# Chunks 0 and 1 of the first expert in turns of four blocks of f, with a later due time for the second group of weights, and another order of the steps between the two experts

## The chip, the cores and the metric

The kernel runs on one core of one Trainium2 chip. The metric is the device time of one execution in microseconds; the median of three runs stands for the kernel, and less is better. The engines are TensorE (PE, the matrix products; its weight loads are shown as PEld), VectorE (DVE), ScalarE (ACT), GpSimd (POOL) and SyncE (SP), which here issues every DMA. Each engine works through its own queue in order.

## The reference

Two batches of 3008 x 256 numbers go through a two-dimensional Fourier transform, of which the real part is kept; the 6016 rows that come out pass through two experts one after the other.

```python
X = np.fft.fft(np.fft.fft(x, axis=1), axis=2).real        # (2, 3008, 256)
x = X.reshape(6016, 256)
h = x @ w_in;  g = h / (1 + exp(-h));  x = g @ w_out       # first expert: w_in 256 x 2048
h = x @ w_in2; g = max(h, 0) + alpha * min(h, 0)           # second expert, alpha per column
out = g @ w_out2
```

The weights come as float64. Everything else is float32.

## The kernel before

**Tiles.** For a real input the rows of the transform come in mirrored pairs, so that half of them, 1504 pairs per batch, are enough. The pairs of a batch are three chunks of 502 columns, six chunks in all (c = 0 to 5). The hidden dimension of 2048 is 16 blocks of 128 (f = 0 to 15). Products are done in fp32r, with every factor split into a high and a low part: high x high, low x high and high x low make three matmuls of one product. The high part is an ACT copy, the low part a subtraction on DVE or POOL.

**Start.** Stage A (`stage_a`, lines 250 to 306) transforms batch 0 along 64 points; its results go through DRAM (`store`, line 297, and `load_y`, line 314) to come back turned. The part of them that chunk 1 needs is stored by `rest(1)` and the part of chunk 2 by `rest(2)`. Stage B (`stage_b`, line 317) does the 47-point part in groups: the matmuls at line 327 fill a PSUM tile, ACT copies the high part of z (line 345), DVE subtracts the low part (line 347). Stage C (`stage_c`, line 351) makes from z the three operands of a chunk: even (ev), odd (od) and the column 128 (ny).

**Weights of the first expert.** They are converted in four groups of four blocks of f: `prep_w1(g)` for W_in, called i0 to i3, and `prep_o1(g)` for W_out, called o0 to o3. `to_f32` (line 174) makes float32 from the two halves of a float64 in one ACT pass (line 183) and four DVE passes (lines 187, 191, 195, 199) on 128 x 512; a group of W_in and a group of W_out have two such pieces each, so 8 DVE passes a group. Then POOL forms sum and difference of W_in (lines 427, 430), ACT makes high parts (lines 434, 452) and POOL low parts (lines 437, 456).

**Rounds.** The first expert runs in 96 rounds, one for each pair (c, f) in `ORDER`. A round issues `eo_mm(i)`: three matmuls for pe (even) and three for po (odd); then `mm2(i-2)`, the second product of the round two earlier (`LAG` = 2): 12 matmuls that add to four accumulators; then `silu_split(i)`: on DVE t = n * w128 + pe (line 570), hp = t + po (line 573) and t - po (line 574), on ACT two silu passes for each of hp and t (lines 577, 578), and `low1(i-1)`, the low parts gl (line 590), in the first 30 rounds both on POOL. When the next round has another chunk, `mm2` empties the four accumulators: by a copy if it is the chunk's first time (two on ACT, line 625, two on DVE, line 623), by an addition on DVE if it is not (four, line 621). Before, chunks 0, 1 and 2 take f 0 to 7 one after the other, then f 8 to 15; chunks 3 to 5 take all 16 at once.

**What sets the order.** `PLAN` gives each kind of side work a stretch of rounds (a, b); `put` spreads its steps evenly over it. A round's steps are issued after its own operations; `leash` ties them to operations of the round before, so that they are not taken earlier. A scheduler works through this order of the program and takes another instruction only where the next one isn't ready by its own reckoning; what it fixes is the order of each engine's queue. Of the tiles, `pm` (PSUM) has four buffers, shared by pe, po and the tiles of stages B and C, `pa` four for the accumulators, `big` twelve in SBUF for raw weights, y, z, the operands and results of a chunk.

**Passage.** The second expert works in 96 pairs n, of which the first two share their time with `mm2` of the last two rounds (lines 942 and 963). A pair's `outer`, `inner`, `seventh` and `fourth` are seven block products of a Strassen-like form, three matmuls of 252 columns each, into PSUM tiles that ACT and DVE empty (e at line 690, u at lines 708 and 714, h at lines 704, 709, 719), followed by the prelu and by `mm4(n-2)`. Its weights are converted during the first expert (`w2`, rounds 50 to 88), combined in `prep_ws` (ws0, ws1), and the second factor is finished in `prep_wo2(g)`: four ACT passes that multiply with a sign (line 542) and the split into high and low (lines 167, 168), for g = 0 to 3. `split_o1(t)` makes and splits the block sums of the first result: four differences (`forms`, line 650) and five splits (`halves`, lines 659, 660) with the low part on POOL.

Of the kernel before, what the change touches and what calls it, by code (L numbers as in the profile page):

```python
# [19 lines left out]
NF = DFF // 128  # L20
NPAIR = S // 2 + 1
CW = 502
NCB = 3
NC = B * NCB
LAG = 2
PLAN = {
# [6 lines left out]
}  # L33
W2_AHEAD = 2
HALF = 252
# [11 lines left out]
FOLD1 = "pppppppppppppppp"  # L47
LOW1 = "vvpvvvvv"
A_SPLIT = (0, 1)
F_PARTS = (0, 8, 16)  # L50
ORDER = [(c, f) for f0, f1 in zip(F_PARTS, F_PARTS[1:]) for c in range(NCB) for f in range(f0, f1)]
ORDER += [(c, f) for c in range(NCB, NC) for f in range(NF)]
WARM = 20
WARM0 = 8
# [67 lines left out]
def fft_moe_kernel(  # L122
# [12 lines left out]
    nc = tc.nc  # L135
# [95 lines left out]
    cx = wp.tile([128, 128], F32R, name="cx")  # L231
# [8 lines left out]
    LAST = {}  # L240
# [67 lines left out]
    def load_y(b, h, kh):  # L308
        w = (K_PARTS[kh + 1] - K_PARTS[kh]) // 2
        if (b, kh) not in Y:  # L310
            Y[b, kh] = big([96, 2, 6, 128], F32, f"y{b}_{kh}")
        src = YS[b, h, kh].rearrange("n (a j k) m -> j (n a) k m", a=4, j=2)
        for j in range(2):
            last = nc.sync.dma_start(Y[b, kh][48 * j : 48 * j + 48, h, :w, :], src[j])
        return last
# [71 lines left out]
    V2 = {}  # L387
# [11 lines left out]
    def load_half(key, src, i, at=None):  # L399
        if key not in RAW:  # L400
            RAW[key] = big([128, 1024, 2], U32, f"raw_{key}")
        at = i * 512 if at is None else at
        t = RAW[key].rearrange("p n t -> p (n t)")
        return nc.sync.dma_start(t[:, i * 1024 : i * 1024 + 1024], src[:, at : at + 512].bitcast(U32))
# [5 lines left out]
    def wo_tiles(lay, g):  # L410
        for j in range(2):
            WO[lay, g, j] = wp.tile([128, 4, 256], F32R, tag=f"wo{g}_{j}", name=f"wo{lay}_{g}_{j}")

    def load_w1(g):
        load_raw(f"i{g}", wi1[0, :, 512 * g : 512 * g + 512], wi1[1, :, 512 * g : 512 * g + 512])

    def load_o1(g):
        load_raw(f"o{g}", wo1[:, 1024 * g : 1024 * g + 1024])
# [112 lines left out]
        return steps  # L531

    def prep_wo2(g):
        def part(h):
            if h == 0:
                wo_tiles(2, g)
            o = (g % 2) * 1024 + h * 512
            v = V2["o", g // 2][:, o : o + 512]
            for q in range(2):
                f = 4 * g + 2 * h + q  # L540
                w = v[:, 256 * q : 256 * q + 256]
                nc.scalar.activation(w, w, AF.Copy, scale=fc[:, 2, f : f + 1])
            hi, lo = (WO[2, g, j].rearrange("p f e -> p (f e)")[:, h * 512 : h * 512 + 512] for j in range(2))
            split(hi, lo, v, nc.gpsimd)

        return [lambda: part(0), lambda: part(1)]


    ACC1 = {}
# [4 lines left out]
    def eo_mm(i):  # L554
        c, f = ORDER[i]
        g, fo = divmod(f, 4)
# [24 lines left out]
    def lo_pool(i):  # L581
        return i < LO_POOL or 52 <= i < 88

    def low1(i):
        if i < 0:
            return
        for s in range(2):
            hi, h = G[i, s]
            lo = work(F32R, f"gl{i}_{s}")
            LAST["gl", i] = (nc.gpsimd if s or lo_pool(i + 1) else nc.vector).tensor_tensor(  # L590
                lo, h, hi.bitcast(F32), op=ALU.subtract
            )
            G[i, s] = (hi, lo)

    def mm2(i, lbs=(0, 1)):
        c, f = ORDER[i]
        g, fo = divmod(f, 4)
# [38 lines left out]
    def split_o1(t):  # L636

        c, s = divmod(t, 2)
        b = lambda k, j: O1[c][:, 2 * s + k, (L, R)[j]]
        box = {}  # L640

        def forms(n):
            if n == 0:
                box["t"] = [work(F32, f"xt{t}_{j}", 2 * HALF) for j in range(2)]
            t1, t2 = box["t"][0][:, :HALF], box["t"][0][:, HALF:]
            t3, t4 = box["t"][1][:, :HALF], box["t"][1][:, HALF:]
            to, p, q = (
                (t1, b(0, 1), b(0, 0)), (t3, b(1, 1), b(0, 1)), (t2, b(1, 1), t1), (t4, b(1, 0), t2),
            )[n]
            nc.gpsimd.tensor_tensor(to, p, q, op=ALU.subtract)  # L650

        def halves(n):
            if n == 0:
                OS[t] = [big([128, 7, HALF], F32R, f"os{t}_{j}") for j in range(2)]
            hi, lo = OS[t]
            to = slice(n, n + 1) if n < 3 else slice(2 * n - 3, 2 * n - 1)
            src = b(*((0, 0), (1, 0), (1, 1))[n]) if n < 3 else box["t"][n - 3]
            hi, lo = (o[:, to, :].rearrange("p b n -> p (b n)") for o in (hi, lo))
            nc.scalar.activation(hi, src, AF.Copy)  # L659
            nc.gpsimd.tensor_tensor(lo, src, hi.bitcast(F32), op=ALU.subtract)  # L660

        return [lambda n=n: forms(n) for n in range(4)] + [lambda n=n: halves(n) for n in range(5)]
# [126 lines left out]
    if True:  # L789
        with tc.manual_schedule():  # L790
            zero = conv(F32, "zero")
            nc.vector.memset(zero[:, :256], 0.0)
            warm(zero[:, :128], zero[:, :256], WARM0)
            nc.vector.memset(sm, 0.0)
            nc.scalar.activation(sm[:1, :1], sm[:1, :1], AF.Silu)
            for j in range(len(PIECES) - 1):
                load_x(0, j, (PIECES[j + 1] - PIECES[j]) // 2)
                if j == 0:
                    nc.sync.dma_start(cs[:, :R0], cst[:, :R0])
            cc = conv(F32, "cc")  # L800
            for g in range(2):
                load_half("i0", wi1[g], g, 0)
                if g == 0:
                    nc.sync.dma_start(cc, cst[:, CD0:])
                    nc.sync.dma_start(w128_raw.rearrange("p n t -> p (n t)"), w128.bitcast(U32))
            nc.sync.dma_start(cs[:, R0:], cst[:, R0:CD0])
            fold, mm, rest = stage_a(0)
            (i00, _), (i01, after_i0) = prep_w1(0)
            for (h, i), n in zip(A_ORDER, A_WARM):
                if h == 0:  # L810
                    fold(i)
                mm(h, i)
                warm(cs[:, FA0 : FA0 + 128], cs[:, :256], n)
            load_half("o0", wo1, 0)
            for h in range(2):
                load_y(0, h, 0)
            load_half("o0", wo1, 1)
            load_w1(1)
            load_o1(1)
            warm(cs[:, FA0 : FA0 + 128], cs[:, :256], WARM)  # L820
            (s0, p0), (s1, p1) = prep_o1(0)
            w128_st = to_f32(lambda: w128_sb, ("w128", 0, NF), "w128")[1]
            run(i00[:4])
            run(i01[:2])
            run(w128_st[:1])
            nc.scalar.activation(ch, cc, AF.Copy)
            run(i00[4:])
            for ab in zip(i01[2:], w128_st[1:]):
                run(ab)
            run(w128_st[4:])  # L830
            nc.vector.tensor_tensor(cl, cc[:, : SG0 - CD0], ch.bitcast(F32)[:, : SG0 - CD0], op=ALU.subtract)
            for n, (st, pool) in enumerate(zip(after_i0, SUM0)):
                (st if callable(st) else st[pool == "v"])()
                if n == 2:
                    run(s0)
            b00, b01 = stage_b(0, 0), stage_b(0, 1)
            run(b00[:2])
            run(b01[:2])
            run(p0)
            run(s1[:EARLY_O0])  # L840
            run(stage_c(0, 0))
            rest(1)
            for h in range(2):
                load_y(0, h, 1)
            nc.sync.dma_start(alpha_sb, alpha)
            rest(2)
            for h in range(2):
                load_y(0, h, 2)
        n1 = NC * NF
        fold, mm, rest = stage_a(1)  # L850
# [8 lines left out]
        def put(a, b, steps):  # L859

            for j, st in enumerate(steps):
                plan.setdefault(a + (b - a) * j // len(steps), []).append(st)
# [45 lines left out]
            put(*PLAN[f"ws{pg}"], steps[:8])  # L908
            put(*PLAN[f"ws{pg}b"], steps[8:])
        for g in range(4):  # L910
            put(*PLAN[f"wo{g}"], prep_wo2(g))
        put(n1 - 5, n1 - 1, split_o1(0))

        for i in range(n1):
            pe, po = eo_mm(i)
# [103 lines left out]
```

## Time and profile before

| | |
|---|---|
| median of 3 runs | 976.97 us (976.53 to 977.37) |
| profiled execution, its own time | 975.78 us |
| span of the profiled execution | 974.0 us |
| PE busy | 953.6 us (98%) |
| DVE busy | 785.1 us (81%) |
| ACT busy | 709.3 us (73%) |
| POOL busy | 424.6 us (44%) |
| DMA | 37.06 MB, mostly in the first 75 us |

The profile is of one execution. Times are microseconds from the start of the span, if not marked ns. A line such as L590 is the line of the code that issued an instruction; `gl<-t,gh` says which tile is written from which. "idle before" is the time in which the engine had nothing to do ahead of an instruction, with the instruction that ended it. PEclk is the share of full speed that was granted to PE. PE's records overlap, since matmuls are pipelined, and a few of them can be missing.

### The profile page before, as it was taken

To read this page: it belongs to the slowest core of one execution; us is meant where nothing else is said; L and a number is where in the kernel's file an instruction comes from. 1 tells how busy PE (TensorE), PEld (TensorE's weight loads), DVE (VectorE), ACT (ScalarE), POOL (GpSimd) and SP (SyncE) were. 2 spreads that over 40 slices of the span, in tenths; PEclk is the share of its full clock that TensorE was granted. 3 is DMA by queue.
4 is the path that set the end of the run, shared out by engine and by line. 5 is a ranking of instruction groups with operands and counts; after the bars stand their busy time and mean duration, and the time that the engine had idled before them with its cause. 6 is when DMAs were issued, how large, how long until landed. Compare 5 with 4: busy or idle time off the path is not lost.

```text
span 974.0 us, 14393 instructions
## 1 busy us (share of the span) xinstructions
PE 953.6 (98%) x5186; PEld 821.7 (84%) x5186; DVE 785.1 (81%) x1319; ACT 709.3 (73%) x1410; POOL 424.6 (44%) x368
## 2 busy tenths in 40 slices
PE   8899999999999999999899999999999999999998
PEld 6578888788788888887789999999999999999997
DVE  5977888787696988997588787887878888787876
ACT  3557677575575757778788787888888888887875
POOL 2576889753257677799522131221222112131200
PEclk9989999999999999999999999999999999999999
DMA  8822000015101110100000000000000000000000
GB/s 269 284 78 87 1 1 22 22 28 174 44 1 60 44 61 27 44 1 1 1 1 22 1 22 23 1 22 1 23 22 1 22 1 22 22 1 22 1 23 21
DMA packets 16615, 37.06 MB, mean 38 GB/s; under 512 B 1824, under 2 KB 11296, under 8 KB 14880
## 3 DMA queue, kind: packets, MB, share of 16 engines
q1 hardware_dynamic: 16544, 36.15, 11.2%
q8 instruction: 40, 0.66, 0.3%
q14 instruction: 31, 0.25, 0.1%
HBM read 26.83 MB, written 9.31 MB: 37 GB/s over the span
## 4 chain that ended last, share of the span: by engine, by line
PE 87%; DVE 3%; POOL 3%; ACT 3%; issue 2%; DMA 0%; SPq 0%; POOLq 0%; DVEq 0%; ACTq 0%
PE a L772 27%; PE ac L674 20%; PE a L614 7%; PE a L616 7%; PE a L612 7%; PE b L674 3%; PE po L562 2%; PE po L564 2%; PE pe L562 2%; PE po L563 2%; PE pe L564 2%; PE pe L563 2%; POOL gl L590 2%; PE psb L327 1%; PE psa L283 1%
## 5 line engine op out<-in xcount | busy, mean ns | idle before, releaser
L772 PE MATMUL a<-gh,wo 128*128 128x502 f32 x768 | 268.2, 391 | 0.0
L772 PEld LDWEIGHTS a<-gh,wo 128*128 128x128 f32 x768 | 145.1, 189 | 23.3
L741 DVE SCALAR_TENSOR_TENSOR h<-h,fc,q 128x502 f32<-128x502 f32 x192 | 129.9, 676 | 38.0 <-ACT q L736 35.3
L590 POOL TENSOR_TENSOR gl<-t,gh 128x502 fp32r<-128x502 f32 x96 | 133.6, 1392 | 55.4 <-ACT t L578 44.5
L614 PE MATMUL a<-gl,wo 128*128 128x502 f32 x384 | 148.6, 396 | 4.0 <-POOL gl L590 2.9
L772 PE MATMUL a<-gl,wo 128*128 128x502 f32 x384 | 149.7, 391 | 0.0
L616 PE MATMUL a<-gh,wo 128*128 128x502 f32 x384 | 146.6, 392 | 0.0
L577 ACT ACTIVATE gh<-hp 128x502 fp32r<-128x502 f32 x96 | 59.8, 623 | 116.5 <-DVE hp L573 115.5
L752 DVE TENSOR_TENSOR gl<-h,gh 128x502 fp32r<-128x502 f32 x192 | 140.7, 733 | 0.1
L612 PE MATMUL a<-gh,wo 128*128 128x502 f32 x384 | 119.2, 393 | 2.4 <-ACT gh L577 2.3
L747 ACT ACTIVATE gh<-h 128x502 fp32r<-128x502 f32 x192 | 118.4, 617 | 2.1 <-DVE h L741 2.1
L590 POOL TENSOR_TENSOR gl<-hp,gh 128x502 fp32r<-128x502 f32 x65 | 90.1, 1386 | 68.1 <-ACT hp L578 66.5
L736 ACT ACTIVATE q<-h,fc 128x502 f32<-128x502 f32 x192 | 116.9, 609 | 2.8 <-DVE h L719 1.5
L650 POOL TENSOR_TENSOR xt<-o 128x252 f32<-128x252 f32 x24 | 16.7, 715 | 187.2 <-ACT q L736 149.8
L614 PEld LDWEIGHTS a<-gl,wo 128*128 128x128 f32 x384 | 73.1, 190 | 21.6 <-POOL gl L590 5.1
L570 DVE SCALAR_TENSOR_TENSOR t<-n,sm,pe 128x502 f32<-128x502 f32 x96 | 70.3, 732 | 25.5 <-PE pe L564 23.6
L612 PEld LDWEIGHTS a<-gh,wo 128*128 128x128 f32 x384 | 71.8, 189 | 18.7 <-ACT gh L577 4.0
L616 PEld LDWEIGHTS a<-gh,wo 128*128 128x128 f32 x384 | 73.1, 190 | 14.6
L772 PEld LDWEIGHTS a<-gl,wo 128*128 128x128 f32 x384 | 72.4, 189 | 7.6
L708 ACT ACTIVATE u<-ac 128x252 f32<-128x252 f32 x96 | 36.6, 381 | 54.2 <-PE ac L674 54.2
L573 DVE TENSOR_TENSOR hp<-t,po 128x502 f32<-128x502 f32 x96 | 64.5, 672 | 13.9 <-PE po L564 6.8
L660 POOL TENSOR_TENSOR os<-o,os 128x252 fp32r<-128x252 f32 x36 | 32.4, 912 | 92.4 <-ACT os L659 92.4
(191 smaller groups left out, 2294.0 us busy)
## 6 DMA issues: line engine op xcount, KB each, us to landing
out_t<-ot SPq DMA_DIRECT2D x24, 251.0 KB, 2.6
x<-in_xs SPq DMA_DIRECT2D x8, 512.0 KB, 5.4
raw_i<-in_wi SPq DMA_DIRECT2D x8, 512.0 KB, 6.2
raw_w<-in_wi SPq DMA_DIRECT2D x4, 1024.0 KB, 5.9
raw_w<-in_wo SPq DMA_DIRECT2D x4, 1024.0 KB, 4.8
raw_o<-in_wo SPq DMA_DIRECT2D x3, 1024.0 KB, 6.8
y<-ys SPq DMA_DIRECT2D x16, 144.0 KB, 3.4
x<-in_xs SPq DMA_DIRECT2D x2, 1024.0 KB, 4.7
```

Source lines behind the costliest of these rows:

```text
L570: nc.vector.scalar_tensor_tensor(t, E128[c], w128_sb[:, f : f + 1], pe, op0=ALU.mult, op1=ALU.add)
L573: nc.vector.tensor_tensor(hp, t, po, op=ALU.add)
L590: LAST["gl", i] = (nc.gpsimd if s or lo_pool(i + 1) else nc.vector).tensor_tensor(lo, h, hi.bitcast(F32), op=ALU.subtract)
L612: nc.tensor.matmul(ACC1[lb, s], hi, G[i, s][0], start=st, stop=False)
L614: nc.tensor.matmul(ACC1[lb, s], hi, G[i, s][1], start=False, stop=False)
L616: nc.tensor.matmul(ACC1[lb, s], lo, G[i, s][0], start=False, stop=sp)
L674: nc.tensor.matmul(to, w, x, start=start and q == 0, stop=q == 2, skip_group_check=True)
L736: nc.scalar.activation(h["q", i][:, to], source(n, part), AF.Abs, scale=coef(n, i, 1))
L741: nc.vector.scalar_tensor_tensor(h[f"h{i}"][:, to], source(n, part), coef(n, i, 0), h["q", i][:, to], op0=ALU.mult, op1=ALU.add)
L747: nc.scalar.activation(hi, H[n][f"h{i}"], AF.Copy)
L752: nc.vector.tensor_tensor(lo, H[n][f"h{i}"], G[n, i][0].bitcast(F32), op=ALU.subtract)
L772: nc.tensor.matmul(ACC2[lb], w[lb][j], x, start=st and first, stop=sp and last)
```

## The change

- `ORDER`: chunks 0 and 1 take turns of four blocks: rounds 0 to 3 are chunk 0 with f 0 to 3, rounds 4 to 7 chunk 1 with f 0 to 3, rounds 8 to 11 chunk 0 with f 4 to 7, rounds 12 to 15 chunk 1 with f 4 to 7; rounds 16 to 23 are chunk 2 with f 0 to 7 as before, and from round 24 on nothing differs.
- `PLAN`: chunk 1's stages B and C stand in rounds 2 and 3 (they were in 4 to 7), i1 in 4 to 7 (1 to 3), o1 in 6 to 9 (4, 5), chunk 2's in 11 to 14 (9 to 14), i2 in 13 to 17 (8 to 13), o2 in 16 to 21 (14 to 18). The loads of i2 and o2 move from rounds 5 and 8 to 9 and 10.
- SP's queue at the start: `rest(1)` is issued ahead of the load of i1, and the load of o1 only behind the y loads of chunk 1.
- `prep_wo2` is cut in two: the signs stand in stretches of their own in rounds 84 to 92, the splits of g = 2 and 3 in rounds 98 to 101 (97 to 99 before), each group's two halves in two rounds.
- `split_o1(0)` stands in rounds 89 to 93 (91 to 94 before).
- Both low parts of the last round go to DVE (one was on POOL).

```diff
@@ PLAN
-    "o0": (1, 2), "i1": (1, 4), "o1": (4, 6), "c1": (4, 8), "cx": (8, 9), "c2": (9, 15),
-    "li2": (5, 6), "i2": (8, 14), "lo2": (8, 9), "o2": (14, 19), "li3": (14, 15), "i3": (19, 24), "lo3": (19, 20), "o3": (24, 29),
+    "o0": (1, 2), "c1": (2, 4), "i1": (4, 8), "o1": (6, 10), "cx": (8, 9), "c2": (11, 15),
+    "li2": (9, 10), "i2": (13, 18), "lo2": (10, 11), "o2": (16, 22), "li3": (14, 15), "i3": (19, 24), "lo3": (19, 20), "o3": (24, 29),
...
-    "wo0": (86, 87), "wo1": (90, 91), "wo2": (97, 98), "wo3": (98, 100),
+    "sg0": (84, 86), "sg1": (87, 89), "sg2": (89, 91), "sg3": (91, 93),
+    "wo0": (86, 88), "wo1": (90, 92), "wo2": (98, 100), "wo3": (100, 102),
@@ ORDER
-F_PARTS = (0, 8, 16)
-ORDER = [(c, f) for f0, f1 in zip(F_PARTS, F_PARTS[1:]) for c in range(NCB) for f in range(f0, f1)]
+ORDER = [(c, f) for f0 in (0, 4) for c in range(2) for f in range(f0, f0 + 4)] + [(2, f) for f in range(8)]
+ORDER += [(c, f) for c in range(NCB) for f in range(8, NF)]
@@ prep_wo2
-        def part(h):
-            if h == 0:
-                wo_tiles(2, g)
+        def signs(h):
...
                 nc.scalar.activation(w, w, AF.Copy, scale=fc[:, 2, f : f + 1])
+
+        def part(h):
+            if h == 0:
+                wo_tiles(2, g)
...
             split(hi, lo, v, nc.gpsimd)
-        return [lambda: part(0), lambda: part(1)]
+        return [lambda: signs(0), lambda: signs(1)], [lambda: part(0), lambda: part(1)]
@@ low1
+        end = i == len(ORDER) - 1
...
-            LAST["gl", i] = (nc.gpsimd if s or lo_pool(i + 1) else nc.vector).tensor_tensor(
+            LAST["gl", i] = (nc.gpsimd if not end and (s or lo_pool(i + 1)) else nc.vector).tensor_tensor(
@@ the start
             load_half("o0", wo1, 1)
+            rest(1)
             load_w1(1)
-            load_o1(1)
...
             run(stage_c(0, 0))
-            rest(1)
             for h in range(2):
                 load_y(0, h, 1)
+            load_o1(1)
@@ the plan
-            put(*PLAN[f"wo{g}"], prep_wo2(g))
-        put(n1 - 5, n1 - 1, split_o1(0))
+            first, then = prep_wo2(g)
+            put(*PLAN[f"sg{g}"], first)
+            put(*PLAN[f"wo{g}"], then)
+        put(n1 - 7, n1 - 2, split_o1(0))
```

## Rows read from the trace of the kernel before

**Rows 1.** The page, its first line: span and number of instructions.

```profile
span 974.0 us, 14393 instructions
```

**Rows 2.** PE's waits, 0 to 130 us: total us, times, longest.

```profile
PE a L612 <- ACT gh L577: 2.3, 2, 1.2
PE pe L562 <- DVE z L347: 1.9, 1, 1.9
...
PE a L614 <- POOL gl L590: 0.9, 2, 0.6
...
PE pe L562 <- ACT wi L434: 0.5, 1, 0.5
PE po L562 <- DVE t L570: 0.3, 1, 0.3
```

**Rows 3.** Windows: length, busy us of PE, PEld, DVE, ACT, POOL, then PEclk.

```profile
41.00:61.00 20.00, 14.25 (x51) 9.75 (x50) 16.79 (x23) 8.67 (x18) 12.87 (x11) 0.86 0.48 170
106.00:140.00 34.00, 33.77 (x148) 27.41 (x147) 32.02 (x43) 22.02 (x41) 26.36 (x20) 1.00 0.00 1
```

**Rows 4.** Timeline of PE: start, duration, line, operation, [idle before <- releaser].

```profile
31.12 0.39 PE L562 MATMUL pe<-eo,wi 128*128 128x502 f32 x1
...
48.82 0.79 PE L562 MATMUL pe<-eo,wi 128*128 128x502 f32 x1 [0.46 <-ACT wi L434]
...
49.82 0.62 PE L616 MATMUL a<-gh,wo 128*128 128x502 f32 x1
```

**Rows 5.** Timeline of POOL, the last low part of i1.

```profile
52.68 1.47 POOL L437 TENSOR_TENSOR wi<-cvi,wi 128x512 fp32r<-128x512 f32 x1
```

**Rows 6.** Timelines of the passage, in order of time.

```profile
460.06 2.93 POOL L660 TENSOR_TENSOR os<-xt,os 128x504 fp32r<-128x504 f32 x2
...
461.38 0.39 PE L674 MATMUL ac<-os,ws_5h 128*128 128x252 f32 x1 [0.35 <-POOL os L660]
...
464.24 0.49 PE L614 MATMUL a<-gl,wo 128*128 128x502 f32 x1 [1.68 <-POOL gl L590]
...
470.25 0.89 ACT L542 ACTIVATE v2o<-v2o,fc 128x256 f32<-128x256 f32 x2
...
471.71 0.57 ACT L690 ACTIVATE e<-ac 128x504 f32<-128x504 f32 x1
...
472.33 0.49 PE L674 MATMUL ac<-os,ws_6h 128*128 128x252 f32 x2 [1.62 <-ACT e L690]
```

**Rows 7.** Windows of tiles t, cvi, cvo (DVE first); copies; L621 in ns.

```profile
31.00:165.00 134.00, 59.66 (x87) 34.65 (x56) 39.31 (x27) 0.97 0.21 69
31.00:165.00 134.00, 21.11 (x24) 5.58 (x9) 11.85 (x9) 0.97 0.21 69
31.00:165.00 134.00, 28.96 (x27) 7.70 (x13) 8.41 (x6) 0.97 0.21 69
...
157.69 1.26 DVE L623 COPY o<-a 128x502 f32<-128x502 f32 x2
...
L621 DVE TENSOR_TENSOR o<-a,o x12: 666/670/680, 186.6 to 265.1; 128x502 f32<-128x502 f32 x12
```

**Rows 8.** SP's timeline, and DMA issues with KB each and us to landing.

```profile
24.06 1.47 SPq L297 DMA_DIRECT2D ys<-ya  x2
...
raw_i<-in_wi SPq DMA_DIRECT2D x2, 512.0 KB, 7.5
...
ys<-ya SPq DMA_DIRECT2D x2, 288.0 KB, 10.3
```

**Rows 9.** Timelines of DVE and POOL, one form of conversion at two times.

```profile
85.74 0.42 DVE L191 TENSOR_SCALAR cvi<-cvi 128x512 uint32<-128x512 uint32 x1
...
105.17 1.47 POOL L590 TENSOR_TENSOR gl<-hp,gh 128x502 fp32r<-128x502 f32 x1
105.55 1.38 DVE L191 TENSOR_SCALAR cvo<-cvo 128x512 uint32<-128x512 uint32 x1
```

**Rows 10.** Window of all engines ahead of the passage, columns as in rows 3.

```profile
444.00:460.00 16.00, 16.00 (x74) 13.28 (x73) 14.13 (x19) 13.21 (x26) 16.00 (x15) 1.00 0.01 2
```

More of the change, by code (lines that the diff above doesn't have):

```diff
@@ L542, in part @@
                 nc.scalar.activation(w, w, AF.Copy, scale=fc[:, 2, f : f + 1])
+        def part(h):
+            if h == 0:
+                wo_tiles(2, g)
+            o = (g % 2) * 1024 + h * 512
+            v = V2["o", g // 2][:, o : o + 512]
             hi, lo = (WO[2, g, j].rearrange("p f e -> p (f e)")[:, h * 512 : h * 512 + 512] for j in range(2))
             split(hi, lo, v, nc.gpsimd)
-        return [lambda: part(0), lambda: part(1)]
+        return [lambda: signs(0), lambda: signs(1)], [lambda: part(0), lambda: part(1)]
     ACC1 = {}
```

## The prediction, made before the change was run

> **What bounds the kernel now.** I read the page's first part, then TensorE's waits, the windows by stage, and the timelines of the two stretches where the waits lie. The span is 974.0 us [rows 1]; the run that was profiled took 975.78, so 1.8 lie outside the span, and the median shown, 976.97, is 1.2 above it. TensorE (PE) works nearly all the time, so a change can only win where PE stands still or runs slowly. In the first 130 us the waits of the rounds are five rows: 2.3, 1.9, 0.9, 0.5 and 0.3, together 5.9 us [rows 2]. The windows place them: from 41 to 61 us PE is busy for 14.25 of 20, at a granted clock of 0.86, so 0.14 x 20 = 2.8 us of cycles are lost too; from 106 to 140 it is busy for 33.8 of 34, with VectorE (DVE) at 32.0 [rows 3]. So this stage loses 5.9 + 2.8 = 8.7 us, and what follows loses nothing. The clock fell while PE kept stopping: matmuls at 49.8 take 0.62 us, on the lower level of 1.2 GHz, where those at 31.1 take 0.39 [rows 4].
>
> What is late there: pe of round 4 waits at 48.82 for the second group of W_in (i1) [rows 4], whose last low part leaves GpSimd (POOL) only at 52.68 + 1.47 = 54.2 [rows 5]. At PE's pace rounds 0 to 3 (six matmuls each, two of them with twelve more, 0.228 us each: 33.77 / 148 [rows 3]) are 48 x 0.228 = 10.9 us, and the rounds begin at 31.1 [rows 4]: i1 was due at 42.
>
> The second place is the passage, 461 to 473: 0.35 and 1.68 behind POOL, 1.62 behind ScalarE (ACT), together 3.65 us [rows 6]. All that the change can give back is about 8.7 + 3.65 = 12.4 us.
>
> **The first 24 rounds.** I count DVE's work against PE's, since DVE is the in-order queue that the weights' conversion and the rounds share. Costs [rows 7]: a round's three operations are 59.66 / 29 = 2.06 us; 51 operations of conversion take (21.11 + 28.96) / 51 = 0.98 each. Neighbours overlap a little (two copies take 1.26, one 0.67), so I take 0.08 off each: 1.82 a round, 0.90 a conversion, 0.59 for a copy or an addition of one accumulator. PE: 6 x 0.228 = 1.37 and 12 x 0.228 = 2.74, 4.10 a full round. Chunk 1's own passes stand in both kernels in this stretch and are left out.
>
> - Before, rounds 0 to 5: 6 x 1.82 + 18 conversions (2 left of o0, 8 of i1, 8 of o1) x 0.90 = 27.1; PE 6 x 1.37 + 4 x 2.74 = 19.2. Excess 7.9, and 8.7 are lost: the count works.
> - After, rounds 0 to 3: 7.3 + 2 x 0.90 = 9.1, and some 3 us for chunk 1, against 11.0 and chunk 1's 3.7 on PE. No excess.
> - After, rounds 4 to 9: 10.9 + 16 x 0.90 + 4 copies x 0.59 = 27.7 against 24.6. Excess 3.1. i1 is due four rounds later, when PE has 16.4 us more behind it.
> - After, rounds 10 to 12: three rounds, hardly more on DVE than 5.5 of 12.3. This slack can't be used, as the steps are tied to their rounds.
> - After, rounds 13 to 21: i2, o2 and i3 now follow on one another, 24 conversions, and chunks 0 and 1 are each closed once more: 8 additions. 9 x 1.82 + 21.6 + 8 x 0.59 = 42.7, with c2's and fa's passes 44.6; PE 9 x 4.10 + 1.8 (c2) = 38.7. Excess 5.9, a new one. Before, rounds 14 to 21 have 16 conversions and 2 copies: 30.2 against 32.8, and nothing was lost.
>
> An excess is lost where PE can't run on. How much it can isn't shown: at least nothing (before, the whole excess was lost), at most one round, 4.1 us (four PSUM buffers hold pe and po of two rounds). I take 2 us, the middle: 1.1 + 3.9 = 5.0 us lost (0 + 1.8 to 3.1 + 5.9 by the bounds). I add 1 us for chunk 1, whose seven PSUM tiles now pass through the four buffers within two rounds, where before it had four: between 0 and the 1.9 that PE waited for z [rows 2]. Lost 6.0 in place of 8.7: **2.7 us won** (bounds 6.9 won to 2.2 lost). The clock is counted in the old 8.7; shorter single waits should leave it high, else up to 2.8 come back.
>
> SP's queue. Chunk 1 must be in SBUF by round 2, near 34 us. The store of its part lands 10.3 us after its issue at 24.1, behind i1 and o1; i1's halves, just ahead of them in the queue, land 7.5 us after their issue [rows 8]. In i1's place the store is issued over 1 us earlier and lands 2.8 us faster, at 30 to 31, and the y loads follow, behind i1's 1 MB: about 34, just in time. They are queued ahead of o1, alpha, rest(2) and y of chunk 2; o1 slips to about 38, and is wanted in round 6, after 50. i2 and o2 are loaded later too, three and six rounds before use: nothing. While SP waits for the store, nothing that is due stands behind it.
>
> Before a new chunk's second products can begin, the four accumulators must be emptied; the two extra changes of chunk I price at 0 beyond DVE's time, which is in the excess (if PE stood still for all four additions of each, 2 x 2.4 us).
>
> **The Trainium skill speaks against this.** Of the conversions the trace shows one and the same form at 0.42 and at 1.38 us [rows 9], the long one inside a low part on POOL. The Trainium skill, SBUF — State Buffer, "Who interferes with whom", says that DVE and GpSimd share a port pair as an exclusive lock: an operation of DVE in a two-port mode, or with two SBUF inputs, that comes second waits until GpSimd's instruction is done, while one with a single SBUF input outside those modes doesn't contend. The trace agrees: the twelve additions, with one input in PSUM, take 0.67 to 0.68 us each [rows 7]. By that rule, with a POOL that never rests, all forty conversions of rounds 4 to 9 and 13 to 21 would come to the 1.38 of [rows 9]: 40 x 0.40 = 16 us more than the sum below, 987; by the mean of [rows 7], which has POOL's share in it, none. Rival 2 stands between.
>
> **The passage.** The halves of split_o1(0) go from rounds 92 to 94 to rounds 91 to 93, its forms to 89 and 90. POOL did its last two lows, 2.93 us, from 460.06, straight ahead of gl of round 94 [rows 6]. With these two rounds earlier, gl (1.3) starts near 460.1 and ends at 461.4; PE wanted it at 464.24 - 1.68 = 462.6. Both POOL waits go, 2.0 us. gl of the last round goes to DVE, one operation of about 1 us, wanted by PE only with the last round's products, behind those of e: 0.
>
> ACT: wo2 in one round is two pairs of signs (0.89 the pair) and two highs of 0.6, 3.0 us in line, and e of the second pair begins at 471.71 behind them [rows 6]. Without them e can begin near 468.7 and end at 469.3, where PE wants it at 472.33 - 1.62 = 470.7. That goes too, 1.6 us. The signs now stand in rounds 84 to 92, eight (3.6 us) more than before, where ACT is busy for 13.2 of 16 us [rows 10]: spread over two such windows that is (26.4 + 3.6) / 32 = 94%, tight, but it fits. wo3 falls into pairs 4 and 5, beside the halves of split_o1(1): I keep 0.25 us back for ACT there. **3.4 us won** (bounds 1.5, if the dearer of the two waits comes back elsewhere, to 3.65).
>
> **Sum.** 975.78 - 2.7 - 3.4 = 969.7 for a run like the profiled one; against the median 1.2 more, 970.9. I predict **971**.
>
> **Rivals.**
> 1. Only the passage pays, the first stage loses elsewhere what it wins: PE runs 0 us ahead of DVE and the excess of 3.1 + 5.9 is lost whole. 976.97 - 3.4 = 973.6. For it: before, nothing of the excess was hidden. Against: DVE at 32.0 of 34 us cost PE nothing [rows 3].
> 2. The other side. DVE's conversions grow dearer in rounds 5 to 9 and 13 to 21, because POOL is denser there: ten lows and six passes of i1 and o1, at 26.36 / 20 = 1.32 us each [rows 3], are 21 us of POOL within the 20.5 of rounds 5 to 9. Forty conversions at 1.25 in place of 0.98 (below the 1.38) are 10.8 us more: 971 + 10.8 = 982. It decides from a mean of about 1.13, where 40 x 0.15 eats the 6.1 won. Against: the mean of 0.98 was already paid beside a POOL that was busy for 26.4 of 34 us.
> 3. More than I expect: PE runs a round ahead of DVE and the later excess vanishes in it. 8.7 - 1.8 - 0.5 = 6.4 and 3.6 won: 967.
> 4. It doesn't do what it says: y of chunk 1 lands after 38, PE stands still in round 4 as before for i1. Some 4 us of waiting more than forecast: 975. Against: the landings worked out above.
>
> **How the numbers follow.** Forecast 0.45, rival 1 0.19, rival 2 0.15, rival 3 0.15, rival 4 0.06. About 0.2%, 2 us, is what a measurement of this kernel can tell from no change. Faster: nearly all of the forecast, rival 1 and rival 3, 0.75; same: rival 4 and the edges of 1 and 2, 0.11; slower 0.14. The likeliest case alone reaches from 967 to 975; with the rivals the range is 965 to 979.
>
> **What would show it.** PE's waits for gh, z and wi between 40 and 60 us gone or under 1 us each, and the clock at 1.0 there; the y loads of chunk 1 issued near 31; c1's matmuls between 34 and 45. New PE waits of 1 to 2 us between 105 and 135 us, behind DVE's hp or t. In the passage no PE wait over 0.5. Wrong if the conversions' mean is over 1.13, if the clock falls again, or if PE waits for chunk 1's eo in round 4.

## The result: 7.6 us slower, and the profile after

The changed kernel takes 984.31 us (983.93 to 984.84, 4 runs) against 976.75 for the kernel before in the same runs (975.65 to 977.37): ratio 1.0078 [1.0065, 1.0090], with its 95% interval. The forecast was 971, in a range of 965 to 979. The profiled execution took 984.84 us, 9.1 more than that of before (975.78). Its page begins with the span, and PE's line in the first part (busy us, share, instructions):

```profile
span 983.0 us, 14408 instructions
PE 958.1 (97%) x5186; PEld 822.7 (84%) x5186; DVE 795.3 (81%) x1328; ACT 709.7 (72%) x1410; POOL 426.4 (43%) x367
```

The lines are 5 to 6 further down than before (L562 is L567, L612 is L618, L614 is L620, L590 is L596). The windows, with the columns of [rows 3], and two stretches more:

```profile
41.00:61.00 20.00, 20.00 (x98) 16.88 (x98) 14.31 (x26) 11.92 (x27) 9.68 (x8) 1.00 0.48 165
61.00:81.00 20.00, 15.49 (x55) 10.50 (x54) 18.48 (x22) 12.62 (x22) 18.69 (x16) 0.91 0.18 56
106.00:140.00 34.00, 31.19 (x127) 24.16 (x125) 32.24 (x42) 19.05 (x35) 23.04 (x17) 0.95 0.09 32
140.00:165.00 25.00, 22.45 (x93) 16.82 (x93) 21.99 (x30) 18.24 (x32) 23.19 (x17) 1.00 0.00 1
```

From 41 to 61 nothing is lost any more. The hole has moved to 61 to 81, and there is a second one from 106 to 165, where [rows 3] had none. PE's waits in 106 to 165 (total, times, longest):

```profile
PE a L618 <- DVE o L627: 2.2, 1, 2.2
PE a L620 <- POOL gl L596: 1.4, 2, 0.8
PE a L618 <- ACT gh L582: 1.0, 1, 1.0
PE po L567 <- DVE t L579: 0.7, 1, 0.7
```

Waits alone don't give what a stretch loses, since slow matmuls and short stops come on top. So I took PE's pace: in each stretch the time less the work of the matmuls that begin in it, at full pace (0.228 us for one of 502 columns, [rows 3]; 0.111 for the small ones of stage B, the median distance from one to the next). Two marks split the rest: the passage is the time from the first product of the second expert's sums (ac) to the issue of the first output. All from the profiled executions, in us; a few matmul records can be missing, so a stretch is good to some 0.5. Two executions differ by more: in e3, e5 and e6 the queues of all engines have the same order up to 411 us, and a stretch still differs by up to 1.8. The kernels of the experiments stand in the same table:

| kernel | 31–61 | 61–81 | 81–111 | 111–171 | passage |
|---|---|---|---|---|---|
| before | 11.1 | 0.7 | 0.4 | 0.3 | 59.0 |
| changed | 1.6 | 7.9 | 0.0 | 9.4 | 61.5 |
| e1 passage only | 10.9 | 0.3 | 0.5 | 3.0 | 61.2 |
| e2 rounds only | 0.9 | 7.7 | 0.6 | 13.5 | 58.8 |
| e3 i2, o2 earlier | 1.1 | 6.8 | 1.8 | 0.5 | 62.7 |
| e4 one closing less | 1.1 | 7.5 | 0.6 | 9.2 | 61.5 |
| e5 e3, old passage | 1.3 | 7.9 | 1.8 | 2.3 | 58.9 |
| e6 e3, two lows on DVE | 1.3 | 7.2 | 1.5 | 2.1 | 57.3 |
| e7 e3, lows on DVE | 1.3 | 5.9 | 4.7 | 0.5 | 61.6 |
| e8 e3, i1 earlier | 3.2 | 1.7 | 5.3 | −0.2 | 62.7 |
| e9 i1 earlier | 2.5 | 1.8 | −0.1 | 7.6 | 61.6 |
| e10 before, passage mended | 11.1 | 0.4 | 0.4 | 0.3 | 57.2 |
| e11 all three | 2.9 | 1.6 | 0.7 | 7.6 | 57.3 |
| e12 all three, spread | 2.7 | 1.7 | 1.9 | 2.3 | 57.2 |
| e14 all three, gaps | 2.9 | 1.8 | 0.9 | 2.1 | 57.6 |

Changed less before: −9.5 + 7.2 − 0.4 + 9.1 in the rounds and 2.5 in the passage, 8.9 of the 9.1.

**The first hole.** The timeline of DVE, with i1's last conversion pass, then that of POOL up to i1's last low part:

```profile
62.53 1.47 DVE L200 SCALAR_TENSOR_TENSOR cvi<-raw_i,cvi 128x512 uint32<-128x512 uint32 x1
```

```profile
65.08 1.48 POOL L428 TENSOR_TENSOR we<-cvi,cvi 128x512 f32<-128x512 f32 x1
66.52 1.45 POOL L596 TENSOR_TENSOR gl<-hp,gh 128x502 fp32r<-128x502 f32 x1
67.92 1.48 POOL L431 TENSOR_TENSOR cvi<-cvi,cvi 128x512 f32<-128x512 f32 x1
69.37 1.69 POOL L596 TENSOR_TENSOR gl<-t,gh 128x502 fp32r<-128x502 f32 x1
71.00 0.75 POOL L883 CAST cx<-cl 128x128 fp32r<-128x128 f32 x1
71.72 1.28 POOL L438 TENSOR_TENSOR wi<-we,wi 128x512 fp32r<-128x512 f32 x1
72.97 1.46 POOL L438 TENSOR_TENSOR wi<-cvi,wi 128x512 fp32r<-128x512 f32 x1
```

DVE is done with i1 at 64.0; its two sums and two low parts then stand between gl and cx, and the last ends at 74.4, 20.2 us later than before (54.2, [rows 5]). The timeline of PE in that stretch:

```profile
69.03 0.39 PE L567 MATMUL pe<-eo,wi 128*128 128x502 f32 x1
71.25 0.97 PE L618 MATMUL a<-gh,wo 128*128 128x502 f32 x2 [1.83 <-ACT gh L582]
72.01 0.62 PE L567 MATMUL po<-eo,wi 128*128 128x502 f32 x1
...
75.41 0.38 PE L568 MATMUL pe<-eo,wi 128*128 128x502 f32 x1
```

At 69.03 the products with i1's high part begin; those with its low part (L568) follow only at 75.41. Between them PE stops for 1.83 us and then runs at the lower level of 1.2 GHz (0.62 in place of 0.39), as it did in [rows 4]. What ends the stop is a gh, whose hp DVE did only at 69.87, behind four passes of o1; e8 and e9 below leave o1 where it is.

**The second hole.** PE's longest stop, and the timeline of DVE around it:

```profile
122.57 0.61 PE L618 MATMUL a<-gh,wo 128*128 128x502 f32 x1 [2.16 <-DVE o L627]
```

```profile
120.22 1.62 DVE L196 SCALAR_TENSOR_TENSOR cvo<-raw_o,cvo 128x512 uint32<-128x512 uint32 x1
121.76 0.67 DVE L627 TENSOR_TENSOR o<-a,o 128x502 f32<-128x502 f32 x1
122.35 0.66 DVE L578 TENSOR_TENSOR hp<-t,po 128x502 f32<-128x502 f32 x1
122.94 1.26 DVE L627 TENSOR_TENSOR o<-a,o 128x502 f32<-128x502 f32 x2
124.11 0.66 DVE L579 TENSOR_TENSOR t<-t,po 128x502 f32<-128x502 f32 x1
124.70 1.65 DVE L200 SCALAR_TENSOR_TENSOR cvo<-raw_o,cvo 128x512 uint32<-128x512 uint32 x1
126.27 1.52 DVE L188 TENSOR_SCALAR cvo<-cvo 128x512 f32<-128x512 f32 x1
127.70 0.67 DVE L627 TENSOR_TENSOR o<-a,o 128x502 f32<-128x502 f32 x1
```

The additions of a closed chunk, the round's own operations and o2's passes take turns without a gap; PE's stop ends with the first addition, which stood behind a pass of 1.62 us, and the fourth comes 6 us after the first. From 120 to 130 the granted clock is 0.83.

**The passage.** Timeline of POOL, and the wait of PE that it causes:

```profile
468.54 1.73 POOL L519 TENSOR_TENSOR ws_7l<-v2w,ws_7h 128x512 fp32r<-128x512 f32 x1
470.23 1.70 POOL L519 TENSOR_TENSOR ws_6l<-v2w,ws_6h 128x512 fp32r<-128x512 f32 x1
471.89 1.24 POOL L596 TENSOR_TENSOR gl<-t,gh 128x502 fp32r<-128x502 f32 x1
```

```profile
473.18 0.49 PE L620 MATMUL a<-gl,wo 128*128 128x502 f32 x1 [2.92 <-POOL gl L596]
```

The two os parts that stood ahead of gl in [rows 6] are gone from there, and two lows of the second expert's slabs stand in their place. The granted clock is 0.87 from 467 to 477, a stretch that holds the stop of 2.92 us.

### The profile page after: what moved, and what is told of

It is laid out like the page before. It is cut to its first block, busy times and chain, and to the rows that moved or that the text cites. A ratio compares the mean times of both kernels' runs of the same rounds, so it can differ in the third digit from the quotient of the medians.

```text
span 983.0 us, 14408 instructions
## 1 busy us (share of the span) xinstructions
PE 958.1 (97%) x5186; PEld 822.7 (84%) x5186; DVE 795.3 (81%) x1328; ACT 709.7 (72%) x1410; POOL 426.4 (43%) x367
## 3 DMA queue, kind: packets, MB, share of 16 engines
q1 hardware_dynamic: 16544, 36.15, 11.1%
## 4 chain that ended last, share of the span: by engine, by line
PE 48%; DVE 2%; ACT 1%; POOL 0%; issue 0%
PE a L778 25%; PE ac L680 19%; PE b L680 3%; DVE h L747 1%; DVE gl L758 1%; ACT q L742 0%; ACT gh L753 0%; DVE h L710 0%; PE a L620 0%; POOL ws_7l L519 0%; POOL ws_6l L519 0%; PE a L622 0%; DVE h L725 0%; PE a L618 0%; POOL gl L596 0%
## 5 line engine op out<-in xcount | busy, mean ns | idle before, releaser
L620 PE MATMUL a<-gl,wo 128*128 128x502 f32 x384 | 150.2, 398 | 7.5 <-POOL gl L596 6.5
L596 POOL TENSOR_TENSOR gl<-t,gh 128x502 fp32r<-128x502 f32 x95 | 132.3, 1392 | 56.3 <-ACT t L583 43.2
L758 DVE TENSOR_TENSOR gl<-h,gh 128x502 fp32r<-128x502 f32 x192 | 144.5, 753 | 0.1
L618 PE MATMUL a<-gh,wo 128*128 128x502 f32 x384 | 120.6, 397 | 5.0 <-ACT gh L582 2.8
L596 POOL TENSOR_TENSOR gl<-hp,gh 128x502 fp32r<-128x502 f32 x65 | 89.5, 1377 | 76.4 <-ACT hp L583 64.5
L620 PEld LDWEIGHTS a<-gl,wo 128*128 128x128 f32 x384 | 73.5, 191 | 27.7 <-POOL gl L596 10.7
L618 PEld LDWEIGHTS a<-gh,wo 128*128 128x128 f32 x384 | 71.9, 191 | 22.2 <-ACT gh L582 5.1
L714 ACT ACTIVATE u<-ac 128x252 f32<-128x252 f32 x96 | 36.7, 382 | 57.8 <-PE ac L680 57.6
```

The lines of the kernel that those rows point to most:

```text
L596: LAST["gl", i] = (nc.gpsimd if not end and (s or lo_pool(i + 1)) else nc.vector).tensor_tensor(lo, h, hi.bitcast(F32), op=ALU.subtract)
L618: nc.tensor.matmul(ACC1[lb, s], hi, G[i, s][0], start=st, stop=False)
L620: nc.tensor.matmul(ACC1[lb, s], hi, G[i, s][1], start=False, stop=False)
L758: nc.vector.tensor_tensor(lo, H[n][f"h{i}"], G[n, i][0].bitcast(F32), op=ALU.subtract)
```

## The experiments

### Which part loses

e1 is the kernel before with the changed passage, e2 the changed kernel with the passage of before:

```
e1: PLAN, ORDER and the load order as before; sg/wo, split_o1(0) and low1 as changed
e2: -put(n1 - 7, n1 - 2, split_o1(0))   +put(n1 - 5, n1 - 1, split_o1(0))
    signs and parts in one step again at the old rounds; end = False
```

> The kernel before with the changed passage alone (signs and parts of the second expert's output weights in steps of their own, split of the first o1 two rounds earlier, last low part of the first expert on VectorE); the rounds of the first stage as before. Theory: the passage is itself about 2.4 us slower, because on GpSimd two lows of the second expert's slabs (1.7 us each) now stand ahead of the low part of round 94; 979.2 us (978.5 to 980). Rival, the working of the prediction: the passage wins 3.4 us, and what was lost there in the changed kernel came from the rounds being late; 973.4.

Measured: 978.8 us, ratio 1.0016 [1.0008, 1.0025]. The passage is itself slower, and its 61.2 us in the table agree. The 3.0 us lost from 111 to 171 are another matter, the long pass told of below: up to 415 us e1's queues have the order of the kernel before, which loses 0.3 there.

> The changed kernel with the passage of the kernel before: only the order and due times of the first stage are changed. Theory: the first stage loses 6.5 us by itself, 983.2 (982 to 984.5), with the waits of the changed kernel between 61 and 165 us. Rival: the first stage wins 2.7 as predicted and the loss belongs to the passage; 974.

Measured: 984.1, ratio 1.0068 [1.0054, 1.0082]. Both parts lose; the rounds lose most. Both rivals fall.

### The second hole: pile-up, or the closings

A closing is the emptying of a chunk's four accumulators, before those of another chunk can be filled.

```
e3: -"li2": (9, 10), "i2": (13, 18), "lo2": (10, 11), "o2": (16, 22)
    +"li2": (7, 8), "i2": (10, 14), "lo2": (9, 10), "o2": (14, 19)
e4: ORDER = (0, f0-3), (1, f0-7), (0, f4-7), (2, f0-7), then as changed
```

> The changed kernel, third group of weights (i2, o2) due in rounds 10 to 14 and 14 to 19 in place of 13 to 18 and 16 to 22, loads two and one rounds earlier; everything else of the change stays, the two extra closings of a chunk too. Theory: the second loss (106 to 165 us) comes from VectorE having i2, o2, i3 and eight additions in nine rounds, and goes for the most part: 978.5 to 980. Rival: it comes from the extra closings themselves (additions in line ahead of the conversions, accumulators not yet empty), whenever the weights are due: 983.5 to 985.

Measured: 977.52, ratio 1.0006 [0.9995, 1.0018]; 6.8 us come back, and in the table 9.4 from 111 to 171 become 0.5 (81 to 111 loses 1.8 more). All eight additions are still there. The windows of e3, columns as above:

```profile
106.00:140.00 34.00, 32.90 (x143) 26.62 (x142) 31.91 (x44) 22.47 (x40) 28.13 (x22) 1.00 0.00 1
140.00:165.00 25.00, 24.68 (x109) 20.14 (x108) 21.52 (x29) 17.90 (x33) 22.39 (x17) 1.00 0.06 22
```

So it is the pile-up of i2, o2, i3 with the additions; the closings by themselves cost little. How full DVE is doesn't tell the three kernels apart: from 106 to 140 it is busy for 32.02 us before [rows 3], 32.24 in the changed kernel and 31.91 in e3.

> The changed kernel with chunk 1's eight blocks in one go: four blocks of chunk 0, eight of chunk 1, the other four of chunk 0, then chunk 2; one closing with its four additions less, and i1 still due in round 8. Theory: VectorE has four passes less in the overloaded stretch, 2.4 us, and the time falls by about as much: 982. Rival, the closing is dear in itself because the accumulators must be emptied before the new chunk's products: half of the second loss goes, 980. Third: closings cost nothing, 984.3.

Measured: 981.0, ratio 1.0039 [1.0026, 1.0052], 3.3 less than the changed kernel. That closings cost nothing falls; 981.0 lies between the theory's 982 and the rival's 980 and decides neither. Its profiled execution has a pass of 6.17 us at 149.15 (below), so the share of the closing itself can't be read from the table.

### The passage

e5 to e8 stand on e3:

```
e5: passage of before (as e2)
e6: -end = i == len(ORDER) - 1    +end = i >= len(ORDER) - 2
```

> The kernel of the run with i2 and o2 due earlier, with the passage of the kernel before. Theory: the parts add up; that run took 977.5, and from the first product of the second expert's sums to the first output it took 62.7 us where the passage of before took 59.0, while the changed passage won 0.8 us ahead of that: 977.5 - 3.7 + 0.8 = 974.6 (973.5 to 975.5), below the kernel before. Rival: the passage depends on what stood before it and its loss stays: 977.5.

Measured: 976.14, ratio 0.9996 [0.9983, 1.0008]. This is above the theory's 973.5 to 975.5 and below the rival's 977.5. The passage takes 58.9, as expected, but 1.8 us more than in e3 are lost from 111 to 171 and 1.1 in the first hole. All queues have the same order in both up to 411 us, so these two are differences between executions and not between kernels.

> i2 and o2 due earlier, with the changed passage, but the last low parts of both last rounds (94 and 95) on VectorE, so that none of them stands behind the lows of the second expert's slabs on GpSimd. Theory: the passage's loss is that order on GpSimd, and it turns into the forecast gain: 977.5 - 3.7 = 973.8 or a little less (972.5 to 975). Rival: the loss of the passage is in what follows (prelu, h and the second expert's slabs being late on GpSimd and ACT): 977 to 978.

Measured: 972.62, ratio 0.9960 [0.9945, 0.9974]: faster than both kernels. With the low parts of rounds 94 and 95 on DVE nothing waits behind the slabs' lows, and the passage takes 57.3. PE's only wait from 450 to 475 is the first row; POOL does the two slabs' lows last, with nobody behind them:

```profile
PE a L620 <- POOL gl L596: 0.9, 1, 0.9
```

```profile
461.25 1.29 POOL L519 TENSOR_TENSOR ws_7l<-v2w,ws_7h 128x512 fp32r<-128x512 f32 x1
462.50 1.72 POOL L519 TENSOR_TENSOR ws_6l<-v2w,ws_6h 128x512 fp32r<-128x512 f32 x1
```

The order on POOL was the cause; the rival falls.

### The first hole: POOL, or the due time

```
e7: -return i < LO_POOL or ...      +return (i < LO_POOL and not 5 <= i < 10) or ...
e8: -"i1": (4, 8), "o1": (6, 10)    +"i1": (2, 6), "o1": (6, 10)
e9: the same edit as e8, on the changed kernel itself
```

> i2 and o2 due earlier, with the changed passage; the first half's low part of rounds 4 to 8 on VectorE in place of GpSimd, five operations of 1.3 to 1.7 us less on GpSimd and about 1 us each more on VectorE. Theory: what makes i1 late in round 8 is GpSimd's queue, full between 62 and 74 us, where i1's two sums and two lows stand between low parts; the 7 us lost from 61 to 81 become 3 to 5, 973.5 to 976. Rival: VectorE is what is late there (i1's last conversion ends only at 63.4), and five more operations on it cost 2 to 4 us more: 979 to 981.

Measured: 978.55, ratio 1.0018 [1.0007, 1.0030], 1.0 worse than e3 by the medians. POOL fell from 19.3 to 13.4 of 20 us between 61 and 81, and the hole only from 6.8 to 5.9; PE then waited 3.0 us at once for a gl on DVE. Neither theory by itself: what leaves POOL's queue arrives in DVE's.

> i2 and o2 due earlier, with the changed passage; i1 due in rounds 2 to 6 in place of 4 to 8, o1 unchanged. Theory: i1 comes two rounds (5.5 to 6 us) sooner through VectorE and GpSimd, since rounds 2 to 4 have room on both, and most of the 7 us lost between 61 and 81 goes: 972 to 974. Rival: the loss is the sum of work on VectorE and GpSimd in rounds 4 to 9 and only moves: 977.

Measured: 976.8, ratio 1.0002 [0.9991, 1.0013]. The hole is nearly gone (6.8 to 1.7; window and i1's last low part below), but 31 to 61 loses 3.2 in place of 1.1, and at 105.8 a new wait of 3.26 us has come: four passes of o2, 0.94 to 1.65 us each, stand ahead of t on DVE. The time is that of the rival, the mechanism that of the theory.

```profile
61.00:81.00 20.00, 19.49 (x84) 14.84 (x82) 18.72 (x25) 15.14 (x28) 19.58 (x17) 1.00 0.15 53
```

```profile
62.22 1.29 POOL L438 TENSOR_TENSOR wi<-cvi,wi 128x512 fp32r<-128x512 f32 x1
```

DVE and POOL are as full as in the changed kernel's window (18.72 and 19.58 against 18.48 and 18.69) and PE loses 0.5 in place of 4.5. So it was not the sum of the work but i1's place in the queues.

> The changed kernel with one thing different: i1 due in rounds 2 to 6 in place of 4 to 8. Theory: the first loss (61 to 81 us, 7.9) comes only from i1 reaching TensorE late, after VectorE's last pass at 64.0 by another 10.4 us of GpSimd's queue; i1 two rounds sooner takes 5 to 6 of it away, the second loss and the passage stay: 979 (978 to 980.5). Rival: the same work in rounds 4 to 16 is only moved, and VectorE's queue gives it back further on: 983 to 985.

Measured: 979.13, ratio 1.0022 [1.0011, 1.0033], 5.2 less than the changed kernel; the hole goes from 7.9 to 1.8, the second loses 7.6 in place of 9.4, and 31 to 61 loses 0.9 more. As the theory had it.

### Mended, on both kernels

```
e10: e1 with the edit of e6
e11: changed kernel with the edits of e6 and e8, and "i2": (10, 14), "o2": (16, 20)
e12: as e11, with i2 (10, 15), o2 (15, 20), i3 (20, 25), o3 (25, 29)
```

> The kernel before with the changed passage, and the low parts of both last rounds on VectorE: the first stage is as before. Theory: the passage as the prediction meant it, with nothing ahead of the low parts of round 94; in the run with i2 and o2 earlier it then won 1.7 us behind the first product of the second expert's sums and 0.8 ahead of it: 977 - 2.5 = 974.5 (973.5 to 975.5). Rival: the pass of 4.96 us at 147.0 that the changed passage alone showed is there again and eats it: 976.5 to 977.5.

Measured: 973.85, ratio 0.9967 [0.9954, 0.9979]. The passage part of the change is worth 3.1 us once nothing stands ahead of gl: the theory, and the rival falls.

> The changed kernel with all three mended: i1 due in rounds 2 to 6, i2 in 10 to 14 and o2 in 16 to 20 (behind chunk 2's passes), low parts of rounds 94 and 95 on VectorE. Theory: the three losses are separate and the repairs add up: 984.3 - 5 - 6.7 - 4.9 = 967.7 (967 to 970). Rival: as where i1 alone was due earlier on top of i2 and o2, a new wait of about 4 us for VectorE's queue takes the place of the first loss: 972.

Measured: 969.79, ratio 0.9929 [0.9914, 0.9944], within the theory's 967 to 970. Two of its six executions took 973.1 and 974.4, the other four 969.4 to 969.9. Only the 974.39 was profiled, and this row stands in it:

```profile
142.83 5.82 DVE L188 TENSOR_SCALAR cvo<-cvo 128x512 f32<-128x512 f32 x1 [1.92 <-ACT cvo L184]
```

> As the kernel with all three mended, with i2, o2, i3, o3 spread evenly: rounds 10 to 15, 15 to 20, 20 to 25, 25 to 29. Theory: VectorE then never has more conversions than TensorE's pace leaves room for, 967 to 969, the same as the other or a little less. Rival: i2's and o2's passes stand beside chunk 2's and the additions of the first closing, and VectorE makes TensorE wait 2 to 4 us there: 970 to 972.

Measured: 972.2, ratio 0.9951 [0.9938, 0.9964], the rival's 970 to 972; 1.9 and 2.3 us are lost from 81 to 111 and from 111 to 171.

### A pass of 5 to 6 us

This row is o3's first pass; the same form takes 0.42 us where nothing is beside it. It is as long in five profiles: 4.96 us in e1, 6.15 in e2, 6.17 in e4, 5.82 here and 4.92 in e15, which is the kernel before with a measurement behind its last output. Up to there every queue of e15 has the order of the kernel before, where the pass took 1.22 (the kernel before, then e15):

```profile
147.56 1.22 DVE L187 TENSOR_SCALAR cvo<-cvo 128x512 f32<-128x512 f32 x1 [1.32 <-ACT cvo L183]
147.15 4.92 DVE L187 TENSOR_SCALAR cvo<-cvo 128x512 f32<-128x512 f32 x1 [1.28 <-ACT cvo L183]
```

So it comes or stays away between executions of one order. In all five DVE had stood idle for 1.28 to 2.02 us before it; in five others with as long an idle time (before, changed, e9, e10, e13) the pass took 1.22 to 1.29. Beside it POOL in e11:

```profile
142.13 1.28 POOL L596 TENSOR_TENSOR gl<-t,gh 128x502 fp32r<-128x502 f32 x1
143.38 1.29 POOL L438 TENSOR_TENSOR wi<-cvi,wi 128x512 fp32r<-128x512 f32 x1
144.63 1.27 POOL L596 TENSOR_TENSOR gl<-hp,gh 128x502 fp32r<-128x502 f32 x1
145.87 1.26 POOL L596 TENSOR_TENSOR gl<-t,gh 128x502 fp32r<-128x502 f32 x1
147.10 1.26 POOL L596 TENSOR_TENSOR gl<-hp,gh 128x502 fp32r<-128x502 f32 x1
150.75 1.27 POOL L596 TENSOR_TENSOR gl<-t,gh 128x502 fp32r<-128x502 f32 x1 [2.39 <-ACT t L583]
```

The pass ends at 148.65, 0.29 us after POOL's line of instructions (148.36); in the other four it ends 0.28 to 0.29 us after the line too. Three more kernels try that:

```
e13, behind the last output: nc.vector.tensor_scalar(x, x, F64_AT_F32_ZERO, None, op0=ALU.max)
    and the other passes, 2 alone, 3 beside 6 x nc.gpsimd.tensor_tensor(g, a, g, op=ALU.subtract)
e14: e11 with LO_POOL = 24 in place of 30
e15: as e13, one pass a line, released by ACT at 12 moments
```

> The kernel before with a measurement behind its last output, of the disputed cost alone: the conversion's passes on VectorE (128x512), two alone and three while GpSimd has six subtractions (128x512, 1.2 to 1.3 us each) in line without a gap; for the pass with a maximum also beside three. Theory: such a pass can be held until GpSimd's whole line is through, not only until its running instruction ends; that is what the passes of 4.96 to 6.15 us at 143 to 153 us are: 0.42 alone, then one of about 7 us beside six and about 3.5 beside three; the pass with two inputs in SBUF likewise or less. Rival: it waits for one instruction of GpSimd at a time, no pass above 1.8 us; then the passes of 5 to 6 us have another cause.

Measured: the timeline has three passes and POOL's line (the first pass, 0.42 us, began ahead of it), and the view by source line each sort of pass with its count and minimum, median and maximum in ns:

```profile
975.83 3.22 DVE L976 TENSOR_SCALAR mx<-mx 128x512 f32<-128x512 f32 x3
976.05 8.14 POOL L974 TENSOR_TENSOR mg<-ma,mg 128x512 f32<-128x512 f32 x6 [58.42 <-DVE ma L983]
```

```profile
L976 DVE TENSOR_SCALAR mx<-mx x10: 412/426/1367, 974.4 to 988.1; 128x512 f32<-128x512 f32 x10
L978 DVE SCALAR_TENSOR_TENSOR mx<-my,mx x5: 684/692/1635, 1001.6 to 1005.9; 128x512 uint32<-128x512 uint32 x5
```

For the line that was measured it is the rival: a pass waits for one instruction of POOL, 0.43 becomes 1.37, and the next one again. But it isn't the kernel's line. Its instructions begin 1.34 to 1.40 us apart in the case shown, each 0.08 us after the one before has ended, where those of e11 above follow every 1.25 us without a gap.

> The kernel before with a second measurement behind its last output: twelve times a line of six subtractions on GpSimd, and beside it one pass with a maximum on VectorE that is released by ACT, after VectorE stood idle, at twelve different moments of the line (0.8 to 2.5 us after its begin, by two to four ACT operations ahead of it). Theory: whether VectorE gets in at the end of GpSimd's running instruction depends on the moment at which it asks: some of the twelve passes take up to 1.8 us, one or more are held to the end of the line, 5 to 7 us, as the passes of o3 were. Rival: all twelve take under 1.8 us, as in the measurement without the idle time, and the cause of the long passes stays open.

Measured: the rival again, 1.27 us at most (view as before), beside lines with the same gaps of 0.08 us.

```profile
L982 DVE TENSOR_SCALAR mx<-mx x12: 427/530/1269, 976.5 to 1075.8; 128x512 f32<-128x512 f32 x12
```

What holds o3's first pass for a whole line in some executions stays open; a line without gaps was not measured by itself.

> The kernel with all three mended, with the first half's low part of rounds 23 to 28 on VectorE in place of GpSimd, so that GpSimd has gaps where o3 is converted. Theory: the pass of 5.82 us at 142.8 is gone (none above 1.8 there) and the time is at or below that kernel's fast runs, 968.5 to 969.8. Rival: VectorE, busy for 22.4 of 25 us from 140 to 165, pays for six more low parts of 1 us what the pass cost: 971 to 973.

Measured: 969.93 (969.23 to 970.37), ratio 0.9918 [0.9903, 0.9933]; the rival's 971 to 973 falls. No conversion pass takes over 1.8 us, and no execution over 970.4; the best version of the study is this one or e11 without the pass. That gaps on POOL take the long pass away fits; but the order on DVE changed with them and the pass no longer follows an idle time, and one profile without it shows little, since it comes only in some executions.

## Why the prediction was wrong, step by step

In the profiled executions I forecast 6.1 us won and 9.1 were lost, a miss of 15.2.

- **What bounds the kernel: right.** The losses of [rows 2, 3] between 31 and 61 us are gone, 11.1 to 1.6, of which chunk 1, taken as 1, can be a part. The 8.7 that I put on this stretch are 11.1 by PE's pace, so the count of an excess of 7.9 fitted less well than it seemed; the stretch came out 1.8 us better than forecast.
- **SP's queue: right.** The y loads were issued at 28.1, ahead of the 31 that I named, c1's matmuls ran from 37.5 to 43.4, and rival 4 falls.
- **"i1 is due four rounds later, when PE has 16.4 us more behind it": the step that failed, 6.1 us of the miss.** Rounds 4 to 9 were to lose 1.1; the stretch loses 7.9 where before lost 0.7. PE's need moved by four rounds, but the due time moved too, from (1, 4) to (4, 8), so i1's low part came 20.2 us later and the lead was used up. I counted DVE's work against PE's as if its order were free, and left out that i1's last 10.4 us, from 64.0 to 74.4, stand in POOL's queue between other work. With the same work two rounds sooner, in e8 and e9, the stretch loses 1.7 and 1.8 (and the one ahead of it 2.1 and 0.9 more); e7 shows that relieving POOL alone is no cure.
- **Rounds 13 to 21: 4.8 of the miss.** The excess was rightly seen (5.9), but I took 2 us as hidden; 9.4 were lost from 111 to 171 where before lost 0.3. The two changes of chunk that I priced at 0 beyond DVE's time are part of it: PE stood still for 2.16 us until the first addition, which waited behind o2's passes, and the clock, 0.95 from 106 to 140, adds 0.05 x 34 = 1.7 us. e3 shows the cause by spreading the same passes: with all additions 0.5 is lost.
- **The price of the conversions: right.** The tiles' windows, DVE first, as in [rows 7]:

```profile
31.00:165.00 134.00, 20.29 (x24) 5.51 (x9) 12.77 (x9) 0.97 0.20 65
31.00:165.00 134.00, 30.09 (x26) 7.53 (x12) 7.39 (x5) 0.97 0.20 65
```

  50.38 / 50 = 1.01 us against 0.98; the forty that rival 2 meant take 1.03 (the same groups 1.00 before), far from its 1.13, so it falls. Only o2's eight grew dearer, 10.6 us from 117 to 139 where they took 8.7 before. The slow side came by another mechanism. The Trainium skill, SBUF — State Buffer, "Who interferes with whom", has an operation of DVE in a two-port mode or with two SBUF inputs that comes second wait until GpSimd's instruction is done: e13 agrees, with 0.43 to 1.37 us a pass for one SBUF input and 0.69 to 1.64 for two (no run shows in which mode the first sort runs). Taken for every pass, it overstates; one pass of 4.92 to 6.17 us in five executions exceeds it.
- **The passage: 5.9 of the miss.** The wait for e is gone, as forecast (1.6). "Both POOL waits go" was wrong: I took out two rows and let the row behind them move up, but POOL's queue is planned anew, and two lows of 1.7 us filled the place. 2.5 us lost in place of 3.4 won; with e10's edit 3.1 are won by the medians, so the size of the gain was about right. The four items come to 6.1 + 4.8 + 5.9 − 1.8 = 15.0 of the 15.2.
- **Rival 1** was nearest for the rounds, but it had 9.0 lost there, where 15.9 came (7.2 − 0.4 + 9.1), and the passage winning.

## What to carry to other kernels

When a need is moved later, don't move the preparation by as much: the gain is the lead, and a due time moved along with the need gives it back. Two rounds of the shift taken back won 5.2 us (e9); leaving the preparation where it was wasn't tried, and earlier work can get in the way of other work, as in e8, where the time hardly moved. Count the whole chain to the last engine (here POOL's sums and low parts), with what stands in its queue. When work is taken out of an in-order queue that a planner fills, ask what it puts there next, and put the operation that others wait for on an engine where nothing can get ahead of it.

## What was unexpected of the hardware

One pass of DVE, 0.42 us alone, took 4.92 to 6.17 us beside four or five instructions of POOL in line without a gap, in five of the seventeen profiles, always o3's first and always after DVE had stood idle, and ended 0.28 to 0.29 us after the line. It makes executions of one order differ: the kernel before lost 0.3 us from 111 to 171, and with the pass, in e15, 3.2. e11's executions, 969.4 to 974.4, fit that, but only the slowest was profiled. The 20 passes that began inside lines with gaps of 0.08 us, behind the kernel, never took over 1.64 us.
